# Folds queued behind an hl, f2's rows in loads of 52, and a first m = 0 taken alone

## The chip, the cores and the metric

The kernel runs on one core of a Trainium2 chip, as one launch. The metric is device time in microseconds (us) of that launch. The core's engines are TensorE (PE, with its weight loads shown as PEld), VectorE (DVE), ScalarE (ACT), GpSimd (POOL) and SyncE (SP), which here only issues DMAs.

## The reference

The input x has 8 sequences of 3136 positions with 256 channels, in fp32. Two blocks follow each other.

```python
X = np.fft.rfft(x, axis=1)
Yr = Xr @ w_r - Xi @ w_i + b_r
Yi = Xr @ w_i + Xi @ w_r + b_i
Y = soft_threshold(Yr, 0.01) + 1j * soft_threshold(Yi, 0.01)
x = np.fft.irfft(Y, n=3136, axis=1)

mixed = np.real(np.fft.fft(np.fft.fft(x, axis=1), axis=2))
u = x + mixed
un = (u - mean(u)) / sqrt(var(u) + 1e-6)
out = u + np.maximum(un @ w_ch1, 0) @ w_ch2
```

The two matrices of the MLP are 256 x 1024 and 1024 x 256.

## The kernel before, in words

**Stages.** 3136 is taken as 64 x 49 (n1, n2), and the FFT as a matmul over n1 and one over n2. A sequence goes through these stages; the names in brackets are those of the profile, which leaves digits off at the end of names.

- f1 (`p1_first` for sequence 0, `p1` for the others) makes the 64-point transform over n1 for the 49 columns n2. Column m and column 49 - m are a pair; m = 0 stands alone. Its input rows are tiles xf, loaded from in_x; its result is copied to ev and stored to a buffer in DRAM, a for sequence 0 (four tensors of 8 frequencies each, a0 to a24) and ad for each other one, with the indices m (25), t, g, u (32), d.
- f2 (`p2_f2`, L573) loads from there, for 8 u at a time (q = 0 to 3), two tiles af. A half h of the tile, at partition 0 or 64, holds the 25 x 2 = 50 rows (m, t) of 4 u (L603). With the tables tff, loaded as 114 partitions (L268, L598), it makes the transform over n2 in many small products of 50 rows (L374, L379), into g_f.
- w (`p2_w`) multiplies by the complex weights (g_w) and thresholds (Y). yt and g2 (g_yt, g_g) transform back, through a buffer bd in DRAM; mix (g_mix, mq) transforms over the channels, through a buffer md.
- norm (`p3_norm`) loads bf and mt, ends the inverse transform with the products g1 (g_g with bf), adds mt, and takes the statistics. tr transposes (g_ut) to uth, utl. `p3_mlp1` (L1055) makes h, then hh on ACT (L1072) and hl, its low part, on VectorE (L1073), for f = 0 to 7; `p3_mlp2` (L1079) multiplies by the second matrix, into o. The six groups of a sequence (seven for the last) have 8 of these f each: 392 in all. An o product needs hl for its second of three matmuls (L164).

fp32 products of the later sequences are made of three with high and low parts (L162 to L165).

**The fold.** From sequence 2 on, f1's products and the g1 products of an earlier group run together on the quarters of the PE array ("quads", L349, L368): the f1 half waits in `waiting` for the g1 half of its key. For that the rows of a pair are added and subtracted on VectorE first, in place in xf: the fold, `va.tensor_add(e, e, o)` (L517) and one more operation (L518). There are 33 of them. xf has two buffers of the tag x4; the load for the next fold is emitted as this one's quads are.

**What sets the order.** Each stage is a generator that yields due times (T = 10000 is a sequence), and a heap takes the earliest. So instructions are emitted in the order of these times; a scheduler that simulates the engines then orders each engine's queue. It prefers what was emitted first, but takes a later instruction when that one is ready first. `tc.issue_after(x)` puts the instructions of a block behind x in their engine's queue. On the chip each queue runs in order. The fold is due at `t - FOLD*T`, where t is the due time of the g1 half, less 1; f of group g is due at `t0 + T3*f/8`, where T3 is a sixth of T. g_f, g_w, g_mix, g_yt, g_g and g_ut share four PSUM buffers (tag g); h and o have two each.

SP issues nearly all DMAs, in order. Each takes one of eight semaphores, and an issue waits until the DMA before it on its semaphore has landed. `behind(key, ...)` puts a DMA behind the one kept under the key in `af_ld`.

**The first sequences.** `p1_first` (L384) loads the 12 chunks of two pairs of sequence 0, and last m = 0 of sequences 0 and 1 together (L406), 64 rows of 512 columns. The first halves go out from SP, the second from ACT (L414). The results are stored to a0 at once; the stores to a8, a16 and a24, and four to ad1 for sequence 1's m = 0 (L444), wait in `later` until the af loads of the q before have been issued (L456). `keep_busy` (L285) gives PE filler products (o_idle). `p1` (L462) does the rest; for b = 2, 4, 6 it takes m = 0 of two sequences in an extra step, k = 6 (L480, L491, L543).

Of the kernel before, what the change touches and what calls it, by code (L numbers as in the profile page):

```python
# [20 lines left out]
D = 256  # L21
# [34 lines left out]
def tables():  # L56
# [23 lines left out]
    for u in range(U):  # L80
# [34 lines left out]
        tf=tf.reshape(128, U, S)[:114],  # L115
# [25 lines left out]
def spectral_block(ctx: ExitStack, tc: tile.TileContext, x, w_ri, b_ri, w1, w2,  # L141
# [123 lines left out]
    def load_tf():  # L265
        yield 0.31 * T
        for s in range(2):
            tff = sb.tile([114, 4, S], F32, tag="tff", bufs=3, name="tff")  # L268
            behind("x", out=tff, in_=c_tf[:, 4 * s:4 * s + 4, :])
            first_tf.append(tff)  # L270
# [73 lines left out]

    def pairs(b, m, n):

        return xv[b][:, m:m + n], xv[b][:, N2 - m - n + 1:N2 - m + 1][:, ::-1]
# [36 lines left out]
    def p1_first():  # L384


        a0 = dr.tile([NM, 2, 2, 8, D], F32, tag="a0", bufs=1, name="a0")
        a8 = dr.tile([NM, 2, 2, 8, D], F32, tag="a8", bufs=1, name="a8")
        a16 = dr.tile([NM, 2, 2, 8, D], F32, tag="a16", bufs=1, name="a16")
        a24 = dr.tile([NM, 2, 2, 8, D], F32, tag="a24", bufs=1, name="a24")  # L390
        ad1 = dr.tile([NM, 2, 2, U, D], F32, tag="ad", bufs=4, name="ad1")
# [11 lines left out]
        slots.append(("Xl", 1, 1, 0))  # L403
        outs.append(("ev", EVB, 1, 0))
        later = [[], [], [], []]
        todo = chunks + [(0, 2)]  # L406
        xfs = []
        for (m, n), (tag, bufs, z, i) in zip(todo, slots):
            if i == 0:
                xf = sb.tile([128, z * 512], F32, tag=tag, bufs=bufs, name="xf")  # L410
            for r, src in enumerate(pairs(0, m, n) if m else (xv[0][:, 0:1], xv[1][:, 0:1])):
                o = xf[64 * r:64 * r + 64, i * 512:i * 512 + 512] if m else xf[0:64, r * D:r * D + D]
                ld = (nc.scalar if r else nc.sync).dma_start(out=o, in_=src).ins
                if not r:  # L414
                    af_ld["x"] = ld
            xfs.append(xf)
        for ci, (m, n) in enumerate(todo):
# [15 lines left out]
            if i == z - 1:  # L433
                mb = m - 2 * i
                nn = m + n - mb
                v = ev[:, :nn * D].rearrange("p (n d) -> p n d", d=D)
                if m == 0:
                    for k, t in enumerate((a0, a8, a16, a24)):
                        o, i_ = t[0].rearrange("t g u d -> (t g u) d"), ev[32 * k:32 * k + 32, :D]
                        if k:  # L440
                            later[k - 1].append((o, i_))
                        else:
                            af_ld["a"] = behind("x", out=o, in_=i_).ins
                    for k in range(4):  # L444
                        o = ad1[0, :, :, 8 * k:8 * k + 8].rearrange("t g u d -> (t g) u d")
                        later[3].append((o, ev[32 * k:32 * k + 32, D:2 * D]))
                    continue
                for k, t in enumerate((a0, a8, a16, a24)):
                    o, i_ = a_rows(t, mb, nn), v[32 * k:32 * k + 32]
                    if k:  # L450
                        later[k - 1].append((o, i_))
                    else:
                        behind("x", out=o, in_=i_)
# [8 lines left out]
    def p1(b):  # L462
# [4 lines left out]
        for i in (b, b + 1)[:1 + (b % 2 == 0)]:  # L467
            if i not in a_dram:
                ad = dr.tile([NM, 2, 2, U, D], F32, tag="ad", bufs=4, name=f"ad{i}")
                a_dram[i] = lambda u, ad=ad: (ad, u)  # L470
        extra = b % 2 == 0
# [8 lines left out]
        order = sorted([(t, k) for k, t in enumerate(times)] + [((times[3] if b == 2 else times[5]) + 0.03 * T, 6)] * extra)  # L480
# [6 lines left out]
        def load(k):  # L487
# [3 lines left out]
            if k == 6:  # L491
                for c in range(2):
                    behind(7, out=xf[0:64, c * D:c * D + D], in_=xv[b + c][:, 0:1])
# [19 lines left out]
        for i, (t, k) in enumerate(order):  # L513
            if not whole(k):
                yield t - FOLD * T
                e, o = xfs[k][:, 0:512], xfs[k][:, 512:]
                va.tensor_add(e, e, o)  # L517
# [6 lines left out]
            xf = xfs.pop(k)  # L524
            if not whole(k):
# [5 lines left out]
            for r in range(2 - (k == 6)):  # L531
                if whole(k):
                    yield t + (F1_STEP if b == 1 else HALF) * T * r
                    g = gtile("g_f1")
                    with tc.issue_after(f2_mm[0, 2, 1]) if b == 1 and k == r == 0 else nullcontext():
                        rows = slice(0, 64 if k == 6 else 128)
                        te.matmul(g, fwd_f[rows], xf[rows, r * 512:r * 512 + 512], start=True, stop=True)
# [3 lines left out]
                (va.tensor_copy if r and whole(k) and b > 1 else sc.copy)(ev, g)  # L541
                v = ev.rearrange("p (n d) -> p n d", d=D)
                if k == 6:  # L543
                    for c in range(2):
                        st_eng.dma_start(out=a_rows(a_dram[b + c](0)[0], 0, 1), in_=v[:, c:c + 1])
# [9 lines left out]
    xt, yt_, tabs = {}, {}, {}  # L555
    w_mm, last_mm, f2_mm, last_mix, g1_mm = {}, [None], {}, {}, {}
# [16 lines left out]
    def p2_f2(b):  # L573


        for q in range(4):
# [6 lines left out]
            for s in range(2):  # L583
                roomy = b == 0 and q == 2
                if roomy:
                    if s == 0:
                        wide = sb.tile([114, 8 * D], F32, tag="mq", bufs=2, name="af")
                    af = wide[:, s * 4 * D:(s + 1) * 4 * D]
                else:
                    af = sb.tile([114, 4 * D], F32, tag="af", bufs=3, name="af")  # L590
# [3 lines left out]
                if not (b == q == 0):  # L594
                    tag, bufs = ("eo", 2) if roomy else ("bev", 3) if b == 0 and q == s == 1 else ("tff", 3)
                    tff = sb.tile([114, 4, S], F32, tag=tag, bufs=bufs, name="tff")
# [18 lines left out]
            for bi in range(2):  # L615
# [439 lines left out]
    def p3_mlp1(b):  # L1055
        for gi, (g0, z) in enumerate(groups[b]):
            t0, T3 = clock3(b, g0)
            w = z * 128
            for f in range(8):
# [16 lines left out]
                hhl[b, gi, f] = hh, hl  # L1076
                done.add(("h", b, gi, f))
# [108 lines left out]
```

## Time and profile before

| | |
|---|---|
| median of three timed runs | 1858.78 us (1852.59 to 1859.8) |
| the profiled execution, its own time | 1851.65 us |
| its span, from the first to the last instruction | 1849.9 us |
| mean granted clock of TensorE | 0.993 |
| busy: PE, DVE, ACT, POOL | 97%, 65%, 44%, 19% of the span |
| moved by DMA | 230.16 MB |

The profile is of one execution. Busy time of PE is modelled at its ends, so a busy PE isn't one at its peak. The granted clock is 1.00 at 2.4 GHz and 0.50 at 1.2 GHz; a stretch between has had some of both. The DMA share is the mean busy share of the core's 16 DMA engines. Where a row has square brackets, they hold the time that the engine stood idle before the instruction and what ended it; what ended it is inferred. The chain of waits is followed back from the last instruction.

### The profile page before, as it was taken

The numbers are of one execution on the slowest core, as the hardware profiler recorded it, in microseconds if no ns is written. First come the engines' busy times: TensorE is split into PE (matmuls) and PEld (weight loads), VectorE is DVE, ScalarE is ACT, GpSimd is POOL, SyncE is SP. The second block draws the span as 40 slices with busy tenths as digits, with TensorE's granted clock in tenths as the row PEclk, the third lists the DMA queues.
The fourth block names the chain that finished last, engine by engine and source line by source line (L and its number), as shares of the span: only waits on it lengthen the run. The fifth ranks groups of instructions, "written<-read, shape, count | busy, mean of one in ns | idle before, by whom it ended". The sixth has DMA issues, their size and how long they took to land.

```text
span 1849.9 us, 39709 instructions
## 1 busy us (share of the span) xinstructions
PE 1803.1 (97%) x15264; PEld 1555.3 (84%) x15264; DVE 1205.3 (65%) x2875; ACT 821.2 (44%) x1755; POOL 351.4 (19%) x746
## 2 busy tenths in 40 slices
PE   8898999999999999999999999999999999999999
PEld 6676888888888888888888888888888889988888
DVE  4766677776576776667767576677657667664443
ACT  3674454444444444444444344444444444322221
POOL 1522222211122211222211122221212222010000
PEclk9999999999999999999999999999999999999999
DMA  7867453453435434364523544245332533141100
GB/s 205 244 215 187 140 161 122 143 160 108 122 128 150 117 104 146 96 167 120 149 91 117 144 140 143 91 137 147 96 111 87 144 88 102 56 136 58 46 24 35
DMA packets 166804, 230.16 MB, mean 124 GB/s; under 512 B 17454, under 2 KB 122040, under 8 KB 166615
## 3 DMA queue, kind: packets, MB, share of 16 engines
q1 hardware_dynamic: 164807, 225.99, 41.8%
q8 instruction: 120, 1.97, 0.5%
q10 hardware_dynamic: 1808, 1.64, 0.3%
q14 instruction: 69, 0.57, 0.1%
HBM read 124.27 MB, written 103.28 MB: 123 GB/s over the span
## 4 chain that ended last, share of the span: by engine, by line
PE 77%; DMA 10%; DVE 7%; SPq 2%; issue 1%; ACT 1%; DVEq 0%; ACTq 0%
PE o L164 9%; PE o L163 9%; PE h L163 8%; PE h L164 8%; PE h L165 8%; PE o L165 8%; PE g_w L163 3%; PE g_f L379 3%; PE g_w L165 3%; PE g_w L164 3%; PE g_yt L871 2%; DMA xf<-in_x 2%; PE g_g L374 2%; DMA bf<-bd 2%; PE g_ut L1047 2%
## 5 line engine op out<-in xcount | busy, mean ns | idle before, releaser
L1073 DVE SCALAR_TENSOR_TENSOR hl<-h,hh 128x512 fp32r<-128x512 f32 x392 | 269.4, 688 | 367.3 <-ACT hh L1072 366.5
L1072 ACT ACTIVATE hh<-h 128x512 fp32r<-128x512 f32 x392 | 234.4, 599 | 470.8 <-PE h L165 448.5
L164 PE MATMUL o<-w2h,hl 128*128 128x256 f32 x1568 | 432.9, 285 | 10.7 <-DVE hl L1073 9.1
L165 PE MATMUL o<-w2h,hh 128*128 128x256 f32 x1568 | 423.2, 279 | 0.0
L163 PE MATMUL o<-w2l,hh 128*128 128x256 f32 x1568 | 403.1, 287 | 0.1
L163 PEld LDWEIGHTS o<-w2l,hh 128*128 128x128 f32 x1568 | 286.5, 189 | 40.9 <-issue 16.5
L164 PEld LDWEIGHTS o<-w2h,hl 128*128 128x128 f32 x1568 | 295.1, 188 | 26.1 <-DVE hl L1073 19.0
L163 PE MATMUL h<-utl,w1h 128*128 128x512 f32 x784 | 314.9, 402 | 1.9 <-DVE utl L157 1.9
L164 PE MATMUL h<-uth,w1l 128*128 128x512 f32 x784 | 311.3, 397 | 0.0
L165 PE MATMUL h<-uth,w1h 128*128 128x512 f32 x784 | 311.2, 397 | 0.0
L165 PEld LDWEIGHTS o<-w2h,hh 128*128 128x128 f32 x1568 | 295.6, 189 | 3.4 <-issue 1.1
L165 PEld LDWEIGHTS h<-uth,w1h 128*128 128x128 f32 x784 | 147.8, 189 | 31.1 <-issue 1.6
L163 PEld LDWEIGHTS h<-utl,w1h 128*128 128x128 f32 x784 | 147.8, 188 | 26.9 <-issue 7.3
L164 PEld LDWEIGHTS h<-uth,w1l 128*128 128x128 f32 x784 | 148.2, 189 | 17.4
L976 POOL TENSOR_SCALAR vv<-ag 128x2 f32<-128x2 f32 x98 | 19.2, 196 | 751.2 <-DVE ag L973 729.5
L728 ACT ACTIVATE r<-g_w,two_t 128x400 f32<-128x400 f32 x128 | 76.2, 595 | 115.2 <-DVE g_w L724 108.9
L160 POOL TENSOR_TENSOR Xl<-xi,Xh 128x400 fp32r<-128x400 f32 (+1 forms) x66 | 68.1, 1035 | 197.8 <-ACT Xh L639 154.7
L724 DVE SCALAR_TENSOR_TENSOR g_w<-g_w,bias,ks 128x400 f32<-128x400 f32 x128 | 81.5, 637 | 32.1 <-PE g_w L165 31.2
L1097 DVE SCALAR_TENSOR_TENSOR ut<-o,rs,ut 128x256 f32<-128x256 f32 x196 | 82.7, 474 | 12.7 <-PE o L165 12.6
L871 PE MATMUL g_yt<-ident,Y 128*100 128x128 f32 x512 | 85.3, 274 | 3.2 <-DVE Y L729 1.5
L802 POOL TENSOR_TENSOR mq<-mq 100x508 f32<-100x508 f32 x28 | 41.2, 1471 | 247.1 <-DVE g_f L366 125.9
L729 DVE SCALAR_TENSOR_TENSOR Y<-g_w,r 128x400 f32<-128x400 f32 x128 | 72.9, 570 | 22.3 <-ACT r L728 20.9
(168 smaller groups left out, 3376.5 us busy)
## 6 DMA issues: line engine op xcount, KB each, us to landing
bd<-bev SPq DMA_DIRECT2D x128, 196.0 KB
out_dram<-ut SPq DMA_DIRECT2D x98, 256.0 KB
bf<-bd SPq DMA_DIRECT2D x96, 256.0 KB
mt<-md SPq DMA_DIRECT2D x192, 128.0 KB
af<-ad SPq DMA_DIRECT2D x112, 200.0 KB
ad<-ev SPq DMA_DIRECT2D x84, 256.0 KB
md<-mq SPq DMA_DIRECT2D x112, 192.0 KB
xf<-in_x SPq DMA_DIRECT2D x78, 128.0 KB
```

The costliest lines, as they stand in the source:

```text
L160: gp.tensor_sub(out_, full, hi.bitcast(F32))
L163: te.matmul(o, lh, rl, start=start, stop=False)
L164: te.matmul(o, ll, rh, start=False, stop=False)
L165: return te.matmul(o, lh, rh, start=False, stop=stop)
L379: mm = te.matmul(*o, start=True, stop=True)
L724: va.scalar_tensor_tensor(gw, gw, bias[:, c, o:o + 1], ks, op0=ALU.add, op1=ALU.add)
L728: ra = sc.activation(r, gw, AF.Relu, bias=lam_t)
L729: ya = va.scalar_tensor_tensor(y[:, o, :, c, :], gw, LAM, r, op0=ALU.add, op1=ALU.min)
L871: te.transpose(gt[:100, (v * 2 + o) * 128:(v * 2 + o + 1) * 128], y[:, o, place].rearrange("p c j -> p (c j)"), ident)
L1072: sc.activation(hh[:, :w], h[:, :w], AF.Relu)
L1073: dv = va.scalar_tensor_tensor(hl[:, :w], h[:, :w], 0.0, hh[:, :w].bitcast(F32), op0=ALU.max, op1=ALU.subtract)
L1097: va.scalar_tensor_tensor(ut[:, j], o[:, j * D:j * D + D], rs[:, j], ut[:, j], op0=ALU.mult, op1=ALU.add)
```

## The change

- The tables tff are stored and loaded as 128 partitions instead of 114 (L115, L268, L596).
- The buffers a and ad get a 26th row m, which is written with a copy of row m = 0: `edge_rows` names rows 0 and 25, and the store reads its source twice. f2 loads 52 rows to each half of af instead of 50 and multiplies 52; the table's rows for the added two are zero.
- `p1_first` takes m = 0 of sequence 0 alone, before the chunks; sequence 1's m = 0 becomes a step k = 6 of `p1(1)`, behind its last chunk. The four stores to ad1 go. `af_ld["a"]` becomes the last store to a0 of the chunks.
- The first fold operation, in all 33 folds but those emitted before any hl, is put behind the hl emitted last.

```diff
-        tf=tf.reshape(128, U, S)[:114],
+        tf=tf.reshape(128, U, S),
...
+    def edge_rows(t):
+        return t[0:NM + 1:NM].rearrange("m t g u d -> (t g u) m d")
...
-        a0 = dr.tile([NM, 2, 2, 8, D], F32, tag="a0", bufs=1, name="a0")
+        a0 = dr.tile([NM + 1, 2, 2, 8, D], F32, tag="a0", bufs=1, name="a0")
...
-        slots.append(("Xl", 1, 1, 0))
-        outs.append(("ev", EVB, 1, 0))
+        slots.insert(0, ("Xl", 1, 1, 0))
+        outs.insert(0, ("ev", EVB, 1, 0))
-        todo = chunks + [(0, 2)]
+        todo = [(0, 1)] + chunks
...
-                    for k in range(4):
-                        o = ad1[0, :, :, 8 * k:8 * k + 8].rearrange("t g u d -> (t g) u d")
-                        later[3].append((o, ev[32 * k:32 * k + 32, D:2 * D]))
...
-        extra = b % 2 == 0
+        own = 1 if b == 1 else 2
+        extra = b % 2 == 0 or b == 1
...
-        order = sorted([(t, k) for k, t in enumerate(times)] + [((times[3] if b == 2 else times[5]) + 0.03 * T, 6)] * extra)
+        order = sorted([(t, k) for k, t in enumerate(times)] + [((times[3] if b == 2 else times[5]) + (1.5 * F1_STEP if b == 1 else 0.03) * T, 6)] * extra)
...
-                va.tensor_add(e, e, o)
+                with tc.issue_after(last_hl[0]) if last_hl[0] is not None else nullcontext():
+                    va.tensor_add(e, e, o)
...
-                        st_eng.dma_start(out=a_rows(a_dram[b + c](0)[0], 0, 1), in_=v[:, c:c + 1])
+                        st_eng.dma_start(out=edge_rows(a_dram[b + c](0)[0]), in_=v[:, c:c + 1].to_broadcast((128, 2, D)))
...
-                        ld = nc.sync.dma_start(out=af[64 * h:64 * h + 50], in_=ad[:, :, h, u:u + 4].rearrange("m t u d -> (m t) (u d)"))
+                        ld = nc.sync.dma_start(out=af[64 * h:64 * h + 52], in_=ad[:, :, h, u:u + 4].rearrange("m t u d -> (m t) (u d)"))
...
-                        rows = slice(64 * h, 64 * h + 50)
+                        rows = slice(64 * h, 64 * h + 52)
...
+                last_hl[0] = dv.ins
```

## Rows read from the trace of the kernel before

**Rows 1.** The page's first part: busy us, share of the span, instructions.

```profile
PE 1803.1 (97%) x15264; PEld 1555.3 (84%) x15264; DVE 1205.3 (65%) x2875; ACT 821.2 (44%) x1755; POOL 351.4 (19%) x746
```

**Rows 2.** Busy time by stage: length; PE, PEld, DVE, ACT, POOL; granted clock, DMA share, GB/s.

```profile
20.00:75.00 55.00, 45.95 (x612) 37.73 (x610) 31.44 (x68) 30.91 (x74) 19.75 (x23) 0.94 0.76 215
75.00:136.00 61.00, 56.00 (x441) 43.85 (x442) 44.70 (x102) 44.84 (x107) 21.36 (x20) 0.94 0.74 224
136.00:200.00 64.00, 55.78 (x424) 46.18 (x424) 40.66 (x96) 27.06 (x60) 14.24 (x31) 0.89 0.71 188
...
300.00:1350.00 1050.00, 1033.12 (x9082) 896.57 (x9081) 720.79 (x1736) 487.77 (x1038) 205.58 (x429) 1.00 0.43 127
...
1600.00:1800.00 200.00, 200.00 (x1333) 174.33 (x1333) 100.61 (x243) 54.28 (x107) 17.52 (x82) 1.00 0.23 67
```

**Rows 3.** PE's waits from 300 us on: us in total, times, longest.

```profile
PE o L164 <- DVE hl L1073: 8.7, 10, 0.9
PE g_w L163 <- DVE mq L798: 2.5, 3, 0.9
PE g_ut L1047 <- DVE bev L904: 1.5, 2, 0.8
```

**Rows 4.** Line 517: what VectorE stood idle for before it: us, times.

```profile
  DMA xf<-in_x: 27.5, 10
  DMA mt<-md: 26.3, 5
```

**Rows 5.** Timeline around the fold of 410.59.

```profile
410.59 0.68 DVE L517 TENSOR_TENSOR xf<-xf 128x512 f32<-128x512 f32 x1
...
411.19 0.68 DVE L1073 SCALAR_TENSOR_TENSOR hl<-h,hh 128x512 fp32r<-128x512 f32 x1
```

**Rows 6.** Timelines of VectorE and PE around 602, and of PE at 283.

```profile
602.64 0.69 DVE L517 TENSOR_TENSOR xf<-xf 128x512 f32<-128x512 f32 x1 [6.38 <-DMA mt<-md]
...
605.56 0.42 PE L163 MATMUL g_w<-Xl,wsh 128*128 128x400 f32 x1 [0.91 <-DVE mq L798]
...
283.66 0.61 PE L374 MATMUL g_g<-bf,inv_f 64*64 64x512 f32 x1 [1.63 <-DVE g_g L366]
```

**Rows 7.** VectorE's groups from 411.1 to 458.7 us, and two timeline rows.

```profile
L1073 DVE SCALAR_TENSOR_TENSOR hl<-h,hh 128x512 fp32r<-128x512 f32 x12 | 8.2, 686 | 9.2 <-ACT hh L1072 9.2
...
433.73 1.04 PE L379 MATMUL g_f<-xf,fwd_f 64*64 64x512 f32 x8
...
457.90 0.68 DVE L1073 SCALAR_TENSOR_TENSOR hl<-h,hh 128x512 fp32r<-128x512 f32 x1
```

**Rows 8.** The chain of waits, to 130 us: start, us, what.

```profile
22.16 6.54 DMA af<-a
...
60.98 6.92 DMA af<-a
...
68.39 5.76 DMA raw_w<-in_w
```

**Rows 9.** Busy time in a stretch with little but af loads moving.

```profile
22.60:24.20 1.60, 1.60 (x9) 1.33 (x8) 1.51 (x3) 1.23 (x2) 0.00 (x0) 1.00 0.62 182
```

**Rows 10.** Timelines of the first 133 us.

```profile
4.63 13.23 PE L426 MATMUL g_f<-xf,fwd 128*128 128x512 f32 x26
...
62.08 3.08 SPq L329 DMA_DIRECT2D ad<-ev  x4
...
123.00 0.36 SPq L547 DMA_DIRECT2D ad<-ev  x1
...
125.41 1.42 SPq L603 DMA_DIRECT2D af<-ad  x4
...
132.08 0.26 PE L374 MATMUL g_f<-tff,af 50*64 50x50 f32 x1
```

**Rows 11.** Timeline of VectorE: the fold of 179.04.

```profile
179.04 0.69 DVE L517 TENSOR_TENSOR xf<-xf 128x512 f32<-128x512 f32 x1 [8.34 <-DMA xf<-in_x]
```

**Rows 12.** PE's groups from 1600 to 1800 us: the longest beside h and o.

```profile
L1047 PE MATMUL g_ut<-ident,ut 128*128 128x128 f32 x68 | 9.9, 272 | 0.0
```

More of the change, by code (lines that the diff above doesn't have):

```diff
@@ L267, in load_tf @@
         for s in range(2):
-            tff = sb.tile([114, 4, S], F32, tag="tff", bufs=3, name="tff")
+            tff = sb.tile([128, 4, S], F32, tag="tff", bufs=3, name="tff")
             behind("x", out=tff, in_=c_tf[:, 4 * s:4 * s + 4, :])
@@ L384, in p1_first @@
     def p1_first():
-        a0 = dr.tile([NM, 2, 2, 8, D], F32, tag="a0", bufs=1, name="a0")
[L388 to L391, printed above, removed]
+        a0 = dr.tile([NM + 1, 2, 2, 8, D], F32, tag="a0", bufs=1, name="a0")
+        a8 = dr.tile([NM + 1, 2, 2, 8, D], F32, tag="a8", bufs=1, name="a8")
+        a16 = dr.tile([NM + 1, 2, 2, 8, D], F32, tag="a16", bufs=1, name="a16")
+        a24 = dr.tile([NM + 1, 2, 2, 8, D], F32, tag="a24", bufs=1, name="a24")
+        ad1 = dr.tile([NM + 1, 2, 2, U, D], F32, tag="ad", bufs=4, name="ad1")
         a_dram[0] = lambda u: ((a0, a8, a16, a24)[u // 8], u % 8)
@@ L410, in p1_first @@
                 xf = sb.tile([128, z * 512], F32, tag=tag, bufs=bufs, name="xf")
-            for r, src in enumerate(pairs(0, m, n) if m else (xv[0][:, 0:1], xv[1][:, 0:1])):
-                o = xf[64 * r:64 * r + 64, i * 512:i * 512 + 512] if m else xf[0:64, r * D:r * D + D]
+            for r, src in enumerate(pairs(0, m, n) if m else (xv[0][:, 0:1],)):
+                o = xf[64 * r:64 * r + 64, i * 512:i * 512 + n * D]
                 ld = (nc.scalar if r else nc.sync).dma_start(out=o, in_=src).ins
@@ L442, in p1_first @@
                         else:
-                            af_ld["a"] = behind("x", out=o, in_=i_).ins
-                    for k in range(4):
-                        o = ad1[0, :, :, 8 * k:8 * k + 8].rearrange("t g u d -> (t g) u d")
-                        later[3].append((o, ev[32 * k:32 * k + 32, D:2 * D]))
+                            behind("x", out=o, in_=i_)
                     continue
@@ L452, in p1_first @@
                     else:
-                        behind("x", out=o, in_=i_)
+                        af_ld["a"] = behind("x", out=o, in_=i_).ins
         done.add(("a", 0, 0))
@@ L491, in load @@
             if k == 6:
-                for c in range(2):
-                    behind(7, out=xf[0:64, c * D:c * D + D], in_=xv[b + c][:, 0:1])
+                for c in range(own):
+                    behind(5 if b == 1 else 7, out=xf[0:64, c * D:c * D + D], in_=xv[b + c][:, 0:1])
             elif whole(k):
@@ L524, in p1 @@
             xf = xfs.pop(k)
+            w = own * D if k == 6 else 512
             if not whole(k):
@@ L536, in p1 @@
                         rows = slice(0, 64 if k == 6 else 128)
-                        te.matmul(g, fwd_f[rows], xf[rows, r * 512:r * 512 + 512], start=True, stop=True)
+                        te.matmul(g[:, :w], fwd_f[rows], xf[rows, r * 512:r * 512 + w], start=True, stop=True)
                 else:
@@ L540, in p1 @@
                 ev = sb.tile([128, 512], F32, tag="ev", bufs=EVB, name="ev")
-                (va.tensor_copy if r and whole(k) and b > 1 else sc.copy)(ev, g)
-                v = ev.rearrange("p (n d) -> p n d", d=D)
+                (va.tensor_copy if r and whole(k) and b > 1 else sc.copy)(ev[:, :w], g[:, :w])
+                v = ev[:, :w].rearrange("p (n d) -> p n d", d=D)
                 if k == 6:
-                    for c in range(2):
-                        st_eng.dma_start(out=a_rows(a_dram[b + c](0)[0], 0, 1), in_=v[:, c:c + 1])
+                    for c in range(own):
+                        st_eng.dma_start(out=edge_rows(a_dram[b + c](0)[0]), in_=v[:, c:c + 1].to_broadcast((128, 2, D)))
                 else:
@@ L595, in p2_f2 @@
                     tag, bufs = ("eo", 2) if roomy else ("bev", 3) if b == 0 and q == s == 1 else ("tff", 3)
-                    tff = sb.tile([114, 4, S], F32, tag=tag, bufs=bufs, name="tff")
+                    tff = sb.tile([128, 4, S], F32, tag=tag, bufs=bufs, name="tff")
                     with tc.issue_after(af_ld["mt" if b else 1 if q == 1 else 3]) if q == 1 or (b == 0 and q == 2) else nullcontext():
```

10 lines of the change are left out of this document (6 added, 4 removed).

## The prediction, made before any run of the changed kernel

> **What bounds the kernel now.** I read the page's first part, then the busy time by stage, then who PE waited for, then the chain of waits for the start. TensorE is busy for 97% of the span, VectorE for 65% [rows 1]; so the time can fall only where PE stands idle, runs filler, or has its lower clock. By stage PE is idle for 55.00 - 45.95 = 9.1 us at 20 to 75 us, 5.0 at 75 to 136, 8.2 at 136 to 200, and 16.9 in the 1050 us after 300 [rows 2]: 39 us, 2% of the run. The three early stages also show a granted clock of 0.94, 0.94 and 0.89, which is time at 1.2 GHz beside 2.4 GHz.
>
> In the steady stretch PE's waits are short and regular: 10 for an hl (8.7 us), 3 for L798 (2.5), 2 for L904 (1.5) [rows 3]. Before its 33 folds VectorE stood idle until a DMA landed, 27.5 us behind in_x alone and 26.3 more put down to mt [rows 4]. Two forms of harm are visible. At 410.59 a fold whose input was long there runs just ahead of an hl, which starts 0.60 us later [rows 5]; the longest of PE's waits for an hl, 0.9 us, are of this kind. At 602.64 the fold had held VectorE for 6.38 us with bev (L904), L796 and L798 queued behind it; PE's 0.91 at 605.56 is for the last of these [rows 6]. The form of 410 stands nine times, 411 to 1288.
>
> At the start the chain runs through DMAs: a store of a, the loads of af, the next store, and so on to raw_w [rows 8]. While the first af loads are nearly alone in flight the DMA share is 0.62, about 10 of 16 engines [rows 9].
>
> **Fold behind an hl.** By the due times a fold is emitted 0.3 group after the due time of hl 3 of the group two before its own (hl 5 where its own group is the first of a sequence). VectorE's queue runs it much earlier: the fold of 410.59 is followed by 12 more hl before the one that it will now stand behind, which starts at 457.90 [rows 7]. Counted so, 30 of 33 folds move, by 1 to 14 hl; the first three stand far enough back already, the one that waited 8.34 us at 179.04 among them [rows 11]. By then every in_x load is long in, so the waits of [rows 4] go. What PE gets back: 9 x 0.60 = 5.4 us of the nine (0.3 of each stays: other VectorE work), the tenth's 0.4, 2.5 behind L798, 1.5 behind L904, and the 1.63 of 283.66, where g_g's marks were queued behind a fold [rows 3, 6]: 11.4 us. What is late next: the moved fold (0.69 + 0.68, the second still only data-bound) stands in front of something else on VectorE, which is 65% busy, so some PE waits return elsewhere. I take 8 of the 11.4. Bounds: 12 gained at best; at worst none, and a loss by the third rival. The load of the next rows waits for the quads that free x4, and those move with the fold; but so does the fold that needs them, so nothing.
>
> **f2's rows 52, tables 128.** PE's f2 products keep their columns, so no PE time. With 10 of 16 engines at work [rows 9], the first four loads of af last until 28.7 (22.16 + 6.54) [rows 8], some 6.2 us of moving; 50 rows in equal shares over 10 are fives, and 52 in equal shares can be fours over 13. With 52/50 of the bytes that is 0.80 of the time, 1.25 us less. There are four such sets, the last at 60.98 [rows 8]; later in the queue the wait is partly others' transfers, so I take 1.0 each, 4 us. Bounds: 0, were it latency alone, to 5. From 300 us on the DMA share is 0.43 [rows 2] and no PE wait names af: nothing. The tables are issued ahead of af and no wait on the chain names them: nothing on their own; they leave the engines that af uses sooner, which stays in the range.
>
> The Trainium skill ("DMA: Bandwidth & Descriptors", Why a DMA increments its semaphore by 16 and not by 1) says that a transfer is split over the largest number of engines up to 16 that divides both outer sizes: 10 for 50 rows, 13 for 52, 16 for 128 and 6 for 114. By that rule a set would cost the 0.80 taken above; the trace agrees as far as the share of 0.62.
>
> **First sequence's m = 0 first and alone.** The stage has 13 matmuls of 512 columns, each in two instructions, in 13.23 us [rows 10]; its last becomes 256 columns at the front. So the last copy moves up by about half of 1.02 us, but the store behind it becomes the larger one of two chunks: -0.3 (bounds -0.9 to +0.7). Of ACT's loads one goes; SP still issues 13. Four stores of sequence 1's m = 0 leave SP's queue at 62.08, where they hold it for 3.08 us ahead of tif, tff, bd and the raw_w load of 68.39 that the chain names next [rows 8, 10]; most of that was waiting for other transfers, so -1 (bounds 0 to -2.5). The doubled edge rows make four stores 64 KB instead of 32, and six of later sequences 256 instead of 128: beside other work, nothing.
>
> Added: sequence 1's own m = 0, one load, a matmul of 256 columns, one ACT copy, one store, now the last store before its af loads. PE's part is what the first stage gave up. Its place costs: those loads go out at 125.41, four issued within 1.42 us, and f2 takes them at 132.08 right behind the last mix product [rows 10]. The store will be 1 to 2 us later than the last one now, of 123.00, the four loads about 1 us quicker: +0.5 (bounds -1 to +2).
>
> Sum of the start: -4 - 0.3 - 1 + 0.5 = -4.8. PE must have the room: 9.1 + 5.0 us idle [rows 2] are more than that, but VectorE is busy 44.7 of 61 us there and will hold some back: **-4**. At 136 to 200 the same loads crowd the queue in front of the in_x rows that held the fold of 179.04 for 8.34 us [rows 11], in a stage where PE is idle for 8.2; I take **-1** (0 to -5, with the clock at 0.89).
>
> **Sum.** -4 - 1 - 8 = -13 us. Against the profiled execution, 1851.65 us (span 1849.9), that is 1838.7. That execution was quicker than the lowest of the three timed runs; their median is 1858.78, and a median is what will be compared, so the forecast is 1858.8 - 13 = **1846 us**. About 0.5%, 9.3 us, is what a measurement here can tell from no change.
>
> **Rivals.**
> 1. *The start gives nothing* (17%). Loads of 200 KB are latency and queueing, not engine time, and VectorE and ACT set 75 to 136 anyway. For it: a load of the last set still took 6.92 us, when much else was in flight [rows 8]. Against: 0.62 in [rows 9] is a plateau of ten engines. Time: -9 from the folds and the gap at 179, 1850. [...]
> 2. *The waits change places* (15%). The fold no longer delays the hl of 411 but another hl, yl or utl, by the same 0.6 us. For it: VectorE's order is made anew as a whole. Only the waits on a DMA before the fold go, and 2 of 11.4 us stay won: -2 - 5 = 1852.
> 3. *The quads wait for the fold: slower* (13%). The products that read xf stood at 433.73, 24 us before the hl of 457.90 ends [rows 7]; they now must come 26 us later, and the whole FFT work of PE with them, since it shares four PSUM buffers. If the queue then puts the quads straight behind the fold, every lateness of hl (0.69) and fold (0.69 + 0.68) falls on PE: 2 us x 30 = 60 at worst, half of that with other work between; 30 less the 13 gained gives about 1875. It decides from the point where the quads start under 1 us after the second fold operation, where those of 433.73 had over 20 us. Against: at 1600 to 1800 PE is busy for all of 200 us [rows 2] though beside h and o no group there has over 9.9 us [rows 12], so it lives without much FFT work.
> 4. *The change does not do what it says*: an order on one engine and tile shapes leave little room for that; the 52 rows could still go over 10 engines, which is the first rival.
>
> **Numbers.** The forecast has 55%. Its own range is 1835 to 1853 (terms at -22 and -6); nine tenths of it lie under 1849.5, where faster by 0.5% begins. With half of the first rival that makes 0.58 faster; the rest of these two, and the second, make 0.30 within 0.5%; the third, where it bites, 0.12 slower. The range reaches from 1831 into the foot of the third rival, 1862.
>
> **What would show it.** Folds without an idle VectorE before them from 257 us on, each behind an hl; the wait of PE for hl after 300 us down from 8.7 to about 3; PE idle after 300 at some 9 instead of 16.9. A DMA share near 0.8 where only af moves; the first f2 after 27 us with its second loads a good microsecond earlier; the af loads of sequence 1 about 4 us before 125.41. Wrong would be: PE waits on L518, quads within 1 us of their fold, or a new wait on af at sequence 1.

## The result, and the profile after

The changed kernel takes **1833.64 us** (median of four runs, 1831.73 to 1835.37); the kernel before took 1857.91 us beside it (1852.59 to 1859.8). The ratio is 0.9874, with a 95% interval of 0.9851 to 0.9897: 1.3% faster. The forecast was 1846 us. The sign was right, and the gain of 24.3 us was almost twice the 13 us put down: 1833.64 lies inside the whole range, 1831 to 1862, and just under the forecast's own, 1835 to 1853.

The profiled execution of the changed kernel took 1835.37 us (span 1833.6 us, granted clock 0.992). It is the slowest of its four runs, while the one of before (1851.65) was quicker than all of its. So the two profiles stand only 1849.9 - 1833.6 = 16.3 us apart, the medians 24.3. The traces can account for the 16.3; the rest comes back under the experiments.

The page's first part; it answers to [rows 1]:

```profile
PE 1796.7 (98%) x15266; PEld 1555.5 (85%) x15266; DVE 1213.8 (66%) x2875; ACT 818.5 (45%) x1756; POOL 354.1 (19%) x746
```

Busy time by stage, columns as in [rows 2]:

```profile
20.00:75.00 55.00, 46.66 (x609) 38.10 (x607) 32.02 (x71) 31.06 (x74) 19.78 (x23) 0.91 0.88 244
75.00:136.00 61.00, 56.17 (x440) 43.83 (x440) 43.76 (x100) 43.76 (x105) 21.35 (x20) 0.94 0.65 198
136.00:200.00 64.00, 51.84 (x405) 42.06 (x400) 37.96 (x91) 27.81 (x61) 14.28 (x31) 0.89 0.77 196
300.00:1350.00 1050.00, 1045.92 (x9266) 914.35 (x9265) 740.60 (x1764) 493.09 (x1056) 211.41 (x440) 1.00 0.45 131
1600.00:1800.00 200.00, 200.00 (x1324) 174.00 (x1323) 97.95 (x232) 52.98 (x103) 17.56 (x82) 1.00 0.22 64
```

The steady stretch, the fourth row, is where it happened: PE's idle time there fell from 16.9 to 4.1 us. The third row went the other way: PE's idle time from 136 to 200 us rose from 8.2 to 12.2.

PE's waits from 300 to 1350 us (answering to [rows 3]) and what VectorE stood idle for before the fold's first operation, now L521 (answering to [rows 4]):

```profile
PE o L164 <- DVE hl L1079: 3.6, 10, 0.7
PE g_yt L877 <- DVE yl L157: 0.3, 1, 0.3
```

```profile
  DMA xf<-in_x: 6.0, 1
  DMA mt<-md: 4.4, 1
```

Before, VectorE's idle time ahead of folds added up to 58.8 us; now two of the 33 folds have any, 10.4 us, and these are the first two of sequence 2, at 154.83 and 180.51. From 267 us on every fold starts directly behind an hl. One of them on VectorE, with its quads on PE:

```profile
421.38 0.69 DVE L1079 SCALAR_TENSOR_TENSOR hl<-h,hh 128x512 fp32r<-128x512 f32 x1 [1.93 <-ACT hh L1078]
421.99 0.68 DVE L521 TENSOR_TENSOR xf<-xf 128x512 f32<-128x512 f32 x1
422.71 0.69 DVE L522 SCALAR_TENSOR_TENSOR xf<-xf 128x512 f32<-128x512 f32 x1
```

```profile
433.45 1.04 PE L383 MATMUL g_f<-xf,fwd_f 64*64 64x512 f32 x8
```

The hl runs first, the two fold operations follow, and the quads that read xf start 433.45 - 423.40 = 10 us later. No wait of PE ends with a fold's second operation.

**Where the 16.3 us are.** Windows of fixed time compare different work. A better cut runs from the first h product of sequence 1 to that of sequence 5, at 406.94 and 1283.83 us before and at 407.59 and 1268.70 after. Length, PE busy, granted clock, DMA share, GB/s; before, then after:

```profile
406.94:1283.83 876.89, 863.99 (x7559) 1.00 0.44 127
```

```profile
407.59:1268.70 861.11, 858.45 (x7559) 1.00 0.45 131
```

The same 7559 matmuls take 15.8 us less, 3.9 us for each sequence. Of that 12.90 - 2.66 = 10.2 us are idle time and 5.5 us are *busy* time. The start adds 407.59 - 406.94 = 0.65 us, and what follows 1283.83 (1268.70) is shorter by 1849.9 - 1283.83 - (1833.6 - 1268.70) = 1.2 us. So the whole difference of the two profiles lies in the steady part. At the start, what the fold gains there (3.7 us by run 1 below) the two other parts took back.

**Busy time that was waiting.** In before, directly behind a wait of PE for an hl:

```profile
741.74 0.39 PE L164 MATMUL o<-w2h,hl 128*128 128x256 f32 x1 [0.92 <-DVE hl L1073]
741.97 0.28 PE L165 MATMUL o<-w2h,hh 128*128 128x256 f32 x1
742.09 0.28 PE L163 MATMUL o<-w2l,hh 128*128 128x256 f32 x1
```

A product of this kind is shown with 0.28 us, but the next starts 0.12 us behind it. A wait is seen as idle time only past the modelled end of the product before it, so about 0.16 us of every wait, and the whole of a shorter one, counts as busy. So idle time shows only a part of a wait.

A count from start to start shows all of it. For each two neighbouring products in the cut, take the distance between their starts, and what it has above the median of that pair of products over both traces. The medians add up to the same, 802.8 us before and 803.2 after. What lies more than 0.06 us above them adds up to 59.9 and 43.9 us, 16.1 apart, and all of that stands at the products that wait for VectorE and right behind them: 9.0 us at the o products that read hl (4.8 of it shown as idle), 1.5 at the o products behind those (none), 3.3 at g_w, which waits for mq (2.5), 1.6 at g_yt (1.0) and 0.8 at g_ut (0.7). Every other kind of product differs by less than 0.2 us. So the 15.8 us are waits for VectorE, and the 5.5 us that are counted as busy are a part of them.

### The profile page after: what moved, and what is told of

Read it like the earlier page. It is cut to its first block, busy times and chain, and to the rows that moved or that the text cites. A ratio compares the mean times of both kernels' runs of the same rounds, so it can differ in the third digit from the quotient of the medians.

```text
span 1833.6 us, 39783 instructions
## 1 busy us (share of the span) xinstructions
PE 1796.7 (98%) x15266; PEld 1555.5 (85%) x15266; DVE 1213.8 (66%) x2875; ACT 818.5 (45%) x1756; POOL 354.1 (19%) x746
## 4 chain that ended last, share of the span: by engine, by line
PE 89%; DVE 6%; DMA 3%; ACT 1%; issue 1%; SPq 0%; ACTq 0%; POOL 0%; DVEq 0%
PE o L163 10%; PE o L164 10%; PE o L165 10%; PE h L163 9%; PE h L165 9%; PE h L164 9%; PE g_f L383 4%; PE g_w L163 3%; PE g_w L165 3%; PE g_w L164 3%; PE g_yt L877 3%; PE g_g L378 3%; PE g_ut L1053 2%; PE g_g L163 2%; PE g_g L165 1%; PE g_g L164 1%
## 5 line engine op out<-in xcount | busy, mean ns | idle before, releaser
L164 PEld LDWEIGHTS h<-uth,w1l 128*128 128x128 f32 x784 | 148.0, 189 | 17.4 <-issue 0.2
L157 DVE TENSOR_TENSOR yl<-g_yt,yh 100x512 fp32r<-100x512 f32 x112 | 76.5, 684 | 17.8 <-ACT yh L888 17.5
```

The lines of the kernel that those rows point to most:

```text
L157: return va.tensor_sub(out_, full, hi.bitcast(F32))
L164: te.matmul(o, ll, rh, start=False, stop=False)
```

## The experiments

Twelve kernels were run, in four groups of 4, 4, 3 and 1. The kernel before was timed beside each group: its medians were 1856.25, 1858.96, 1854.25 and 1857.31 us. Changes are against the kernel before unless said otherwise; kernels of different groups are set side by side behind run 12.

**1. The fold alone.**

```diff
-                va.tensor_add(e, e, o)
+                with tc.issue_after(last_hl[0]) if last_hl[0] is not None else nullcontext():
+                    va.tensor_add(e, e, o)
```

> The kernel before with the fold's first operation behind the last hl, and nothing else. If the fold carries the steady stretch by itself, PE's idle time from 300 to 1350 us falls from 16.9 to about 4 us, and the time by 12 to 14 us (ratio about 0.993). If the larger loads are needed for it as well (the fold's input late by DMA), the idle time stays above 8 us and the gain under 8. The start, to 136 us, should be as before.

Measured: 1830.97 us (1829.7 to 1831.71), ratio 0.9865 (0.9843 to 0.9887). This one line carries the whole gain, and is 2.7 us better than the whole change (4.3 by their traces). The 4 us of idle time came as expected; the gain, expected at 12 to 14 us, was 25. The stretch from 300 to 1350 us (length, busy, clock, DMA share, GB/s):

```profile
300.00:1350.00 1050.00, 1045.84 (x9267) 1.00 0.44 130
```

PE's idle time is 4.2 us, as after the whole change; the cut from sequence 1 to 5 takes 861.2 us, again the same.

**2. Everything but the fold** (the changed kernel with the fold free).

> The changed kernel with the fold free, as before. If the start's gain survives to the end, 5 to 11 us less than before (ratio 0.994 to 0.997), with PE's idle time after 300 us still near 17. If what the start gains by 60 us is lost again by 150, as the two traces at hand suggest, no difference within 3 us. Fold alone and this one should add up to the whole 24 us if the parts are independent.

Measured: 1859.26 us (1852.77 to 1864.61), ratio 1.0012 (0.9997 to 1.0027). The two other parts together give nothing that shows.

**3. The kernel before once more**, with no edit, as a measure of the noise.

> The kernel before once more, for a second trace. Its first trace was of an execution of 1851.65 us while most runs took 1857 to 1860. If the 6 us between them lie in the start (stalls and the clock's low stretches up to 200 us), a trace of a slower execution shows them there, and 300 to 1350 us as before with 16.9 us idle. If they are spread over the steady stretch, idle time there is above 20.

Measured: 1857.03 us (1852.49 to 1859.1), ratio 1.0004 (0.9992 to 1.0017). Its trace is of an execution of 1853.0 us, 4 below that median, with 17.1 us of PE idle time from 300 to 1350 us; so where the 4 us lie isn't shown.

**4. Rows of 52 and tables of 128 alone**; m = 0 stays last and with sequence 1's.

```diff
-ld = nc.sync.dma_start(out=af[64 * h:64 * h + 50], ...)
+ld = nc.sync.dma_start(out=af[64 * h:64 * h + 52], ...)
...
+                    later[3].append((a_rows(ad1, NM, 1), ...))
```

> The kernel before with rows of 52 and tables of 128 alone; m = 0 stays last, with one store more for sequence 1's added row. The second f2 loads of the first set land about 1.3 us earlier after their issue (4.9 us instead of 6.9), the af loads of the third set 2 us earlier. Time: 3 to 6 us less if the loads are what the start's gain rests on; 0 to 2 if it rests on m = 0 taken first.

Measured: 1848.04 us (1846.13 to 1848.44), ratio 0.9953 (0.9936 to 0.9971): 8 us. Its trace is only 3.5 us shorter than that of before, and of these 0.4 are there at the first h of sequence 1 (406.54 against 406.94); why the medians lie further apart stays open. Run 2 has the same loads and none of the 8 us, so the first m = 0 alone must cost about as much. No run takes the rows of 52 without the tables of 128.

**5. The first m = 0 alone, by itself.**

```diff
-        todo = chunks + [(0, 2)]
+        todo = [(0, 1)] + chunks
...
+        extra = b % 2 == 0 or b == 1
```

> The first sequence's m = 0 alone and first, sequence 1's m = 0 as an item of its own, on the kernel before; rows stay 50, tables 114, folds free. Theory that this part costs by itself: the whole change without the fold stands 11 us above the rows and tables alone (1859.3 against 1848.0), so this one lies about 11 us above the kernel before of the same job, and its trace has sequence 1's af loads issued 2 to 3 us later than before (125.4 us there). Rival, that it costs only together with the broader loads: within 3 us of the kernel before.

Measured: 1868.22 us (1863.24 to 1878.85), ratio 1.0044 (1.0028 to 1.0061), 9.3 us slower. The first theory is near in its size (11 us) and wrong in its mechanism: the af loads of sequence 1 went out at 125.23 us, no later than before. PE reached f2 earlier and waited for them, and then for other things; from its waits from 130 to 200 us:

```profile
PE g_w L163 <- DVE Y L728: 4.6, 1, 4.6
...
PE g_w L163 <- DVE Xsl L157: 1.9, 1, 1.9
PE g_f L379 <- DMA af<-ad: 0.7, 1, 0.7
```

All three kernels with this part (run 2, run 5 and the whole change) have these three waits: 0.7 to 0.9 on af, 1.9 to 2.2 on Xsl, 3.3 to 5.1 on Y. Before and run 4 show none of them. But the wait on Xsl is no loss: that product starts at 138.14 us here, and at 140.65 before, where PE ran filler (o_idle) until then. What puts PE behind is the wait on Y, and VectorE's queue shows why. Before, and then here:

```profile
149.11 0.57 DVE L729 SCALAR_TENSOR_TENSOR Y<-g_w,r 128x400 f32<-128x400 f32 x1 [1.10 <-ACT r L728]
149.60 0.68 DVE L157 TENSOR_TENSOR utl<-g_ut,uth 128x512 fp32r<-128x512 f32 x1
151.64 0.69 DVE L517 TENSOR_TENSOR xf<-xf 128x512 f32<-128x512 f32 x1 [1.36 <-DMA xf<-in_x]
```

```profile
151.65 0.69 DVE L515 TENSOR_TENSOR xf<-xf 128x512 f32<-128x512 f32 x1 [4.33 <-DMA mt<-md]
...
153.62 0.57 DVE L728 SCALAR_TENSOR_TENSOR Y<-g_w,r 128x400 f32<-128x400 f32 x1
```

The first fold of sequence 2, which waits for its rows, now stands ahead of this Y. It does so in the three kernels with this part and in no other. The first h of sequence 0 starts at 156.42 us instead of 153.04.

The second half of the loss lies further on, at a free fold:

```profile
279.90 0.69 DVE L515 TENSOR_TENSOR xf<-xf 128x512 f32<-128x512 f32 x1 [4.34 <-DMA af<-ad]
```

```profile
281.25 0.89 PE L870 MATMUL g_yt<-ident,Y 128*100 128x128 f32 x4 [3.53 <-DVE utl L157]
```

The utl that PE waited for stands right behind this fold, and behind the gap of 3.53 us PE had 6.8 us at 1.2 GHz (granted clock 0.89 from 270 to 300 us; 1.00 before). By the first h of sequence 1 run 5 is 8.0 us behind (414.91 against 406.94). Run 2 has the same gap; the whole change, whose folds from 267 us on wait for nothing, has not. That accounts for the part costing more with free folds than with folds in order.

**6. The fold, with rows and tables**; without the first m = 0 alone (runs 1 and 4 together).

> The fold's order together with the 52-row loads and the 128-row tables, m = 0 left last and with sequence 1's. If the parts add (1831.0 for the fold alone, 8 us for rows and tables alone): 1823 us, and under both. Rival, that what the start gains is met again by 150 us whatever the fold does: 1829 to 1832, no better than the fold alone.

Measured: 1829.25 us (1827.57 to 1830.84), ratio 0.9826 (0.9804 to 0.9848). That is 1.7 us below the fold alone (1.8 by their traces), where run 4 had won 8. The parts do not add: the second expectation came true.

**7. Sequence 2's folds due later** (on top of the fold's order).

```diff
-                yield t - FOLD * T
+                yield t - (FOLD if b > 2 else 0.01) * T
...
+                behind_op = last_hl[0] or ends.get("t", (None, None))[1]
...
```

> The fold's order alone, and sequence 2's three folds due 0.04 of a period later, the first of them behind the first utl operation. In the run with the fold alone two of them still kept VectorE idle for 1.7 us (153.8) and 7.5 us (180.4), beside TensorE gaps of 2.3 and 4.2 us. Theory that an idle of VectorE ahead of a fold is what costs, wherever it is: these two go, TensorE's idle time from 136 to 200 us falls by 3 to 6 us and the time to 1825 to 1828 us. Rival, that this stage waits for its transfers anyway: the gaps move to another wait there and the time stays at 1829 to 1832 us.

Measured: 1829.39 us (1827.69 to 1830.17), within the rival's 1829 to 1832. But VectorE's idle time ahead of folds did not go; it fell from 9.3 us in run 1 to 4.4. The fold met at 180 us still came before its rows (VectorE, then PE):

```profile
180.53 0.69 DVE L519 TENSOR_TENSOR xf<-xf 128x512 f32<-128x512 f32 x1 [4.37 <-DMA af<-ad]
```

```profile
183.09 0.67 PE L874 MATMUL g_yt<-ident,Y 128*100 128x128 f32 x2 [3.17 <-DVE bev L907]
```

PE's idle time from 136 to 200 us fell by 1.8 us (10.8 to 9.0), where 3 to 6 had been expected. So the run didn't decide: this fold was moved by less than its transfer is late.

**8. Folds due later, free.** The constant FOLD from 0.05 to 0.02.

> The kernel before with one constant changed: folds due 0.02 instead of 0.05 of a period ahead of their quads, some 6.5 us later, and no order against any hl. Theory that a fold costs because it waits for its transfer at the head of VectorE's queue: the transfers have landed when the later folds are met, VectorE's idle ahead of folds falls from 58.8 to under 20 us, TensorE's idle from 300 to 1350 us from 16.9 to 4 to 7 us, time 1832 to 1840 us. Rival, that the place right behind an hl is what matters, since a fold ahead of an hl delays it by its own 0.6 to 1.2 us: idle stays at 12 us or more and the time above 1848 us.

Measured: 1858.98 us (1854.55 to 1869.74), ratio 1.0003 (0.9984 to 1.0023). The edit missed its aim. VectorE's idle time ahead of folds was 62.2 us, no less than 58.8; its two largest parts, and the form of [rows 5] again:

```profile
  DMA xf<-in_x: 38.7, 11
  DMA mt<-md: 18.0, 3
```

```profile
413.34 0.68 DVE L517 TENSOR_TENSOR xf<-xf 128x512 f32<-128x512 f32 x1
413.95 0.68 DVE L1073 SCALAR_TENSOR_TENSOR hl<-h,hh 128x512 fp32r<-128x512 f32 x1
```

So 6.5 us in the due time do not keep the fold from standing early; the likely reason, not tested, is the scheduler's rule that it takes what its simulation finds ready. In these runs only an order held the folds back.

**9. One fold on GpSimd.** On top of run 6, the fold of 180 us alone:

```diff
+                if (b, k) == (2, 2):
+                    gp.tensor_add(e, e, o)
+                    gp.tensor_scalar(o, o, -2.0, 0.0, op0=ALU.mult, op1=ALU.add)
+                    gp.tensor_add(o, o, e)
...
```

> The fold's order with the 52-row loads, and in addition one single fold, sequence 2's second (met at 180 us, where VectorE sat idle for 7.5 us in the run with the fold alone), given to GpSimd as three operations. Theory that an idle of VectorE ahead of a fold holds the work queued behind it wherever it is: TensorE's gap of 3.7 us at 177 us goes, and with it perhaps the stretch at half clock behind it, so 1823 to 1826 us. Rival, as with sequence 2's late folds, that another wait takes its place in this stage: 1828 to 1831 us.

Measured: **1821.56 us** (1820.88 to 1822.67), ratio 0.9822 (0.9805 to 0.9839), 7.7 us below run 6, with one fold of 33 moved. The two stand in different groups, and each against the kernel before beside it they have the same ratio; it is the traces that show a difference, 7.5 us at the first h of sequence 1 (393.95 against 401.42). Of these, 2.1 are there at the first h of sequence 0 (151.52 against 153.64), ahead of the moved fold, and are not explained; 5.4 come behind it. Run 12, the same edit on run 11, has 6.0 us in that stretch, and 5.0 by medians. VectorE and PE in run 6:

```profile
178.38 0.69 DVE L524 TENSOR_TENSOR xf<-xf 128x512 f32<-128x512 f32 x1 [7.03 <-DMA mt<-md]
```

```profile
180.81 0.53 PE L163 MATMUL g_g<-yl,tih 100*98 100x256 f32 x1 [3.68 <-DVE yl L157]
```

GpSimd and PE here:

```profile
177.66 1.29 POOL L524 TENSOR_TENSOR xf<-xf 128x512 f32<-128x512 f32 x1 [9.92 <-DMA mt<-md]
```

```profile
186.18 0.45 PE L163 MATMUL g_w<-Xsl,wrh 128*128 128x400 f32 x1 [1.10 <-POOL Xsl L160]
```

Busy time from 136 to 200 us, columns as in [rows 2], in run 6 and here:

```profile
136.00:200.00 64.00, 55.06 (x418) 44.78 (x416) 40.25 (x96) 26.47 (x56) 13.88 (x31) 0.89 0.76 191
```

```profile
136.00:200.00 64.00, 57.65 (x456) 47.80 (x455) 42.63 (x103) 28.71 (x60) 17.23 (x34) 0.97 0.75 192
```

PE's idle time fell by 2.6 us, its gap of 3.7 us at 177 us was gone, and the granted clock rose from 0.89 to 0.97: the 6.8 us at 1.2 GHz that began at 179.9, within that gap, were gone too. In the same 64 us PE did 38 more matmuls. The wait itself is still there: GpSimd now stands idle for 9.9 us ahead of this fold, and all that PE pays is 1.1 us for an Xsl in GpSimd's queue. This is the clearest sign for the theory: VectorE's queue no longer stands behind the rows, and the gap is gone, though the fold still waits for them.

**10. All folds on GpSimd**, the three operations of run 9, free.

> The kernel before with every fold on GpSimd (three operations instead of two), in no order against any hl. Theory that the cost is VectorE's queue, in which a fold stands ahead of an hl: no hl waits for a fold any more, TensorE's idle from 300 to 1350 us falls from 16.9 to 4 to 7 us, and the time is 1828 to 1838 us. Rival, that the order in which the planner writes TensorE's queue is what the constraint improved, or that the waiting folds hold GpSimd's own Xl, mq and Y operations in the same way: idle 12 us or more, time above 1848 us.

Measured: 1849.99 us (1846.58 to 1852.48), ratio 0.997 (0.9959 to 0.9981). The rival's numbers, 17.4 us of idle time from 300 to 1350 us, and most of the gain not there. But the way is one that neither theory named. VectorE before, then VectorE, GpSimd and PE here, around 739 us:

```profile
739.74 0.75 DVE L800 TENSOR_TENSOR mq<-mq 100x256 f32<-100x256 f32 x2
```

```profile
737.25 1.81 DVE L801 TENSOR_TENSOR mq<-mq 100x256 f32<-100x256 f32 x2
738.98 0.68 DVE L1074 SCALAR_TENSOR_TENSOR hl<-h,hh 128x512 fp32r<-128x512 f32 x1
```

```profile
737.34 1.44 POOL L519 TENSOR_TENSOR xf<-xf 128x512 f32<-128x512 f32 x1
```

```profile
739.72 0.38 PE L164 MATMUL o<-w2h,hl 128*128 128x256 f32 x1 [1.87 <-DVE hl L1074]
```

The fold's last operation on GpSimd (737.34 to 738.78) overlaps the two mq operations on VectorE, which take 1.81 us; before, the same pair took 0.75 us. The hl behind them was 1 us later, and PE waited 1.87 us for it, twice the 0.9 of before [rows 3]. This happens at six of the nine places: an mq operation that starts while a fold's operation runs on GpSimd takes 1.3 to 1.5 us, and PE waits 1.6 to 1.9 us for the hl, 10.8 of the 17.4 us in all. At the other three the fold's operation starts behind the first mq operation or at most 0.06 us ahead of it; there the mq operations take 0.42 us each, GpSimd's takes 1.7 to 2.0 us, and PE waits 0.3 us. The Trainium skill ("SBUF — State Buffer", Who interferes with whom) says that a VectorE instruction with two SBUF inputs contends with a GpSimd instruction that reads SBUF, and that the order of issue decides which of the two is held; the rows agree. So a fold off VectorE's queue can still hold VectorE.

**11. The whole change, with sequence 1's m = 0 earlier**: behind its third item instead of its sixth.

```diff
-... ((times[3] if b == 2 else times[5]) ...
+... ((times[3] if b == 2 else times[2] if b == 1 else times[5]) ...
```

> The whole change with one due time moved: sequence 1's own m = 0 behind its third item instead of behind its sixth. Theory that the first m = 0 alone costs because sequence 1's m = 0 is the last store ahead of that sequence's af loads: these are issued at about 125.5 us again instead of 128.0, the waits of TensorE on af (0.9 us) and on Xsl (2.0 us) at 133 to 139 us go, and the time is 1829 to 1830.5 us, as with rows and fold without it. Rival, that one item more in this stage costs wherever it stands: 1832 to 1836 us, as the whole change.

Measured: 1828.4 us (1826.91 to 1829.56), ratio 0.9856 (0.9839 to 0.9873), 5.2 us better than the whole change (5.7 by their traces). The af loads of sequence 1, in the whole change and here:

```profile
128.04 1.15 SPq L609 DMA_DIRECT2D af<-ad  x3
```

```profile
125.30 1.56 SPq L609 DMA_DIRECT2D af<-ad  x4
```

The waits on af and Y are gone, that on Xsl fell from 2.0 to 0.4. So it is the place of that item that costs, not the item. Run 5 had its af loads on time and lost as much, so late af loads are the smaller part. The larger is the order in VectorE's queue: here the first fold of sequence 2 stands behind that Y and a utl again, at 152.81, as in the kernel before. Why the scheduler turns the two round when the item stands last was not tested.

**12. The whole change with both repairs** (runs 9 and 11).

> The whole change with two repairs: sequence 1's own m = 0 behind its third item, and sequence 2's second fold on GpSimd. If the repairs add (the first took 5.2 us from the whole change, 1833.6 to 1828.4; the second took 7.7 us from fold and rows, 1829.3 to 1821.6): 1820.7 us. If the first m = 0 alone is worth nothing and only harmed by its second item's place: 1821.6 us as the fold with rows and one fold on GpSimd; above 1824 us if the two repairs meet in the same stage.

Measured: 1823.45 us (1820.08 to 1825.33), ratio 0.9813 (0.9795 to 0.9831). Run 9's range lies inside this one's: once mended, the first m = 0 alone is worth nothing that shows. Both kernels are 1.8 to 1.9% faster than the kernel before, and 10 to 12 us faster than the whole change.

**Across the groups.** Between the groups the median of the kernel before moved by up to 4.7 us, so two kernels from different groups are compared by their traces beside the medians. For the seven kernels with folds in order the two agree: from the first h product of sequence 1 to the end all seven take 1425.7 to 1426.0 us, and they differ in when that product starts.

| folds in order | median, us | first h of sequence 1, us |
|---|---|---|
| whole change | 1833.64 | 407.59 |
| run 1 | 1830.97 | 403.25 |
| run 7 | 1829.39 | 402.58 |
| run 6 | 1829.25 | 401.42 |
| run 11 | 1828.4 | 401.87 |
| run 12 | 1823.45 | 394.65 |
| run 9 | 1821.56 | 393.95 |

## Why the prediction was right, and where its sizes failed

**Fold behind an hl: right in mechanism, mis-sized.** The step said that 30 of 33 folds move behind an hl, that the waits of [rows 4] go, that PE gets back 11.4 us, and that 8 of them stay, "so some PE waits return elsewhere". The 30 folds moved as counted and wait for nothing now; the 10.4 us that are left stand at two of the three that were not to move. The 0.3 us that was to stay at each of the nine stayed: nine waits of 0.32 us make up most of the 3.6 above. The size failed in both of its halves, and the 15.8 us of the steady part lie above the bound of "12 gained at best". Nothing returned elsewhere: idle time from 300 to 1350 us is 4.1 us and not "some 9". And 11.4 us was too small a base, by the premise that time can fall only where PE stands idle, runs filler or has its lower clock: it was summed from rows of idle time, and the same waits also held 5.5 us of busy time. Between two profiles the fold alone is worth 1849.9 - 1829.2 = 20.7 us: 3.7 before the first h of sequence 1 (406.94 against 403.25), 15.7 in the next four sequences, 1.3 behind them.

**The medians.** By medians the fold alone is worth 25 us. The runs of a kernel with free folds lay 2 to 16 us apart (11.6 for the 24 of before beside run 1); those of a kernel with folds in order 2 to 5, though these had 4 or 5 runs and most of the others 7 to 24. One source is visible: the sequences from 1 to 4 took 219.8, 219.5, 219.0 and 218.6 us in before, and 218.9, 218.4, 219.8 and 221.1 in run 3 of the same program; with folds in order they took 214.8, 215.8, 214.8 and 215.8 in the whole change and the same within 0.1 in run 1. The reading that a transfer which lands early or late no longer moves the time, once nothing on VectorE waits for it, fits these rows; that it is all of the spread was not tested. The forecast was right to be set on the median of before, and wrong to carry the gain over from one profile unchanged. The lower end of its own range doesn't follow from its terms either: 1858.8 - 22 is 1836.8, not 1835.

**Rows 52 and tables 128: right in mechanism, mis-sized.** The loads do use more engines. A stretch like that of [rows 9], and the chain's loads of af, which stood at 6.54 us for the first set [rows 8]:

```profile
22.20:23.80 1.60, 1.60 (x9) 1.33 (x8) 1.51 (x4) 1.23 (x2) 0.00 (x0) 1.00 0.73 227
```

```profile
21.29 3.58 DMA af<-a
...
31.24 4.70 DMA af<-a
...
42.00 4.88 DMA af<-a
```

The DMA share is 0.73 instead of 0.62, at 227 GB/s instead of 182, so rival 1's premise, that it is latency alone, is out. A share "near 0.8" it is not, but the loads' packets of 4 KB tell the same: in these two stretches most often 10 of them are under way at once before and 13 after. By the rule of the Trainium skill ("DMA: Bandwidth & Descriptors", Why a DMA increments its semaphore by 16 and not by 1) 50 rows go over 10 engines and 52 over 13; the traces agree with it. What came of it is less than 4 us. The last two loads of the fourth set go out at 58.37 to 60.00 us with 50 rows (before, runs 1, 3 and 5) and at 56.68 to 58.32 with 52 (whole change, runs 2, 4, 6 and 11); the g_g products behind the raw weights start at 64.48 to 64.94 and at 62.25 to 64.50, 1.2 us earlier in the mean. In the whole change nothing is left at 93 us: the g_g products of 92.04 us before start at 92.81. The f2 products just ahead of them were still 1.2 us earlier (87.69 against 88.90), but from 85.9 to 92.7 us the granted clock was 0.50, which is 6.8 us at 1.2 GHz. Behind the same wait of 2.0 us for an ev, before had 3.4 us of it and run 6 none; what decides that, these runs don't show. In run 6 the same g_g products start at 90.46, and 1.8 us stay to the end. So the step was right in its mechanism, and "-4" is the term that was mis-sized: 1.8 us with the fold in order, and none in the whole change.

**First m = 0 first and alone: mis-sized.** "+0.5 (bounds -1 to +2)" for sequence 1's own m = 0 was the worst step: the part costs 9.3 us alone and 4.4 on top of the fold and the rows (1833.64 against 1829.25; 6.2 by their traces). Of its terms for sequence 0, "-0.3" is too small to tell (the first load of af goes out at 20.88 to 21.89 us with this part and at 20.86 to 22.00 without), and without the four stores that raw_w does go out earlier, at 62.28 to 65.50 us instead of 66.02 to 68.39 ("-1"). The af loads did not come "about 4 us before 125.41" but 2.6 us behind it, and the forecast's own sign of an error, a new wait on af at sequence 1, is there:

```profile
134.42 0.39 PE L383 MATMUL g_f<-tff,af 52*64 52x50 f32 x12 [0.85 <-DMA af<-ad]
```

The step looked at one store, its landing and four loads. It did not follow the item into the next stage, 136 to 200 us, where the larger part was lost. At the products that read bf PE is 1.0 us behind run 1 (146.34 against 145.30), at the first h of sequence 0 it is 4.4 (159.51 against 155.14): the first fold of sequence 2 stands ahead of a Y that PE needs.

```profile
154.83 0.69 DVE L521 TENSOR_TENSOR xf<-xf 128x512 f32<-128x512 f32 x1 [4.37 <-DMA mt<-md]
```

PE waits 3.3 us for the Y behind it, the same harm as in [rows 6], made by the change itself. There "-1" became 4 us more idle time. Together the start's terms, -5 in the forecast, are +4.3 against the fold alone at the first h of sequence 1 (407.59 against 403.25).

**The rivals.** Rival 1, the start gives nothing, happened as to its effect and not by its reason. Rival 2, the waits change places, did not: no new wait of PE over 0.3 us in the steady part. Rival 3, quads that wait for the fold, did not: from 257 us on the lead over the second fold operation is 5 us or more everywhere. A steady part forecast at half its gain and a start forecast with a gain that wasn't there offset each other in part in the profiles, -16.3 against -13 us, and that is luck; the medians show the rest.

## What to carry to other kernels

An operation that waits for a transfer on an in-order queue costs whatever stands behind it; if its own consumer is 10 us away, order it behind the operation that others wait for, or give it to a queue on which nobody waits, after a look at what that engine shares with its neighbour. Size such a gain by cutting the trace at the same products in two executions, since idle time shows only the part of a wait that outlasts the modelled end of the product before it. When an edit moves work from a quiet place into a crowded one, follow it through the next stage, and look at the order of the queues there: here one item more put a waiting fold ahead of work that PE needed.

## What was not expected of the hardware

- Two VectorE additions with both inputs in SBUF took 1.81 us beside a GpSimd addition (run 10), and 0.75 us in the kernel before, without it.
- A gap of 3.7 us in front of PE came with 6.8 us at half clock. With both gone (run 9) the granted clock from 136 to 200 us was 0.97 instead of 0.89, and the stretch from the first h of sequence 0 to that of sequence 1 was 5.4 us shorter, more than the gap; in run 12 against run 11 it was 6.0 us.
- A PE product of 128x256 is shown with 0.28 us while the next starts 0.12 us behind it, so a wait shows as idle time only in part: of 16.1 us of waits that went, 9.0.
